# Converting a float64 weight inside an attention stage: half chunks through a spare PSUM bank, and one multiply moved from VectorE to GpSimd

## The chip, the cores and the metric

One Trainium2 chip, one of its cores. The time is device time of one launch in microseconds (us), from three runs of the kernel before: 694.91, 696.65 and 696.79, median 696.65. One more execution was profiled: it took 696.35 us, of which the profile's span covers 694.6.

## The reference, cut to what matters

The program is a chain of three blocks on a batch of 4 with 576 positions: attention with 8 heads of 64 and rotary position, then a gated feed-forward block, then a mixture of four attention experts.

```
scores = q_rot @ k_rot.T / 8                     # per batch and head, 576 x 576
attn   = exp(scores - max); attn /= sum
x      = attn @ v, heads side by side            # (4, 576, 512)
h      = gelu(x @ w_in)                          # w_in: (512, 1024), float64
u, v   = halves of h; v = layernorm(v) * g_ln
x      = x + (u * (w_sg @ v + b_sg)) @ w_out
out    = sum over the 2 experts chosen of 4 of  w_e * causal_attention_e(x)
```

The input `w_in` comes as float64. The kernel turns it into float32 itself, with integer operations on the two 32-bit words of each number, and then splits each float32 into a high and a low part, so that products on TensorE keep float32 accuracy.

## The kernel before, in words

There are three stages, one for each block. Stage 1 is the one touched. It walks through 16 *works*, one for each batch and pair of heads, and each work has nine *slots*, numbered x = 0 to 8, one for each tile of 128 query rows of the pair. A loop over k = 9n + x calls `slot(k)`, which writes the instructions of work n, slot x, and of its neighbours, in an order fixed by hand on the compute engines; on the queue of the DMA engines (SP) a scheduler may still move transfers.

In slot x TensorE makes the scores of tile x+1 (tile `ps_S`, two buffers), then turns the exponentials of tile x-1 with four transposes (`ps_t`). VectorE takes the maximum of the scores (`nmax`), ScalarE the exponential (`e`). ScalarE and VectorE share the copies of the turned tiles to SBUF (`g`). TensorE multiplies them with the values into `ps_o` in slots 1, 3, 5, 7 and 8.

576 keys are four blocks of 128 and 64 leftover keys. The leftover keys of two tiles are put side by side and turned into a bank of their own, `ps_l` (one buffer): `turn_left` in slots 4, 5 and 7, and in slots 0 and 1 of the work after. `place_left` copies the bank to SBUF (`tl`) in slot 5 and in slot 2 of the work after; the factors of the normalization pass through the same bank (`rr`). From slot 2 to slot 4 and from slot 5 to slot 7 the bank holds nothing that is still wanted.

Queries and keys of the next work are prepared beside this: rotary position on GpSimd (`rope`, tile `t`), a cast to the high part on VectorE (`hi`), the low part on GpSimd (`lo`), in slots 1 (queries) and 3 (keys), and then ten transfers that lay the parts out for TensorE (`q`, `qz`, `kh`). Scores of the next work wait for them.

In the gaps stage 1 does work for stage 2, by generators that are advanced by one step in chosen slots:

- `load_split64` (L226) converts `w_in` in eight chunks of 128 x 512 numbers. One buffer (`raw`) takes the words, one (`wt`) the result. Its steps for a chunk: an absolute value on ScalarE (L245), then on VectorE a maximum (L247), a shift left (L249), an OR with the shifted low word (L251) and an OR with the sign (L255), then the split (`wih` on ScalarE, `wil` on GpSimd) and the transfer of the next chunk. All of it lies in SBUF. The loop (L625) takes one step in slots 1, 3, 4, 6, 7 and 8 of odd works and in slot 7 of even ones.
- `attended` (L289) fetches finished attention outputs (`sa`) and their factors (`sr`), multiplies them (`norm`, L299, for batch 0 on VectorE, else on GpSimd), stores them and splits them. It takes a step in slot 8 of works 4 to 15.

Of the kernel before, what the change touches and what calls it, by code (L numbers as in the profile page):

```python
# [8 lines left out]
F32 = mybir.dt.float32  # L9
# [8 lines left out]
P = 128  # L18
# [17 lines left out]
VALUES_AT = (2, 5, 7)  # L36
FIRST_QK_AT = (0, 1, 3, 3, 4, 4)
GATES_AT = {8: 1, 9: 2, 10: 2, 11: 3}
INPUT_AT = ((0, 1, 2, 4, 6, 7), (1, 3, 5, 7), (2, 4))


@with_exitstack
def fused_kernel(ctx, tc, qk, v, w_in, w_out, w_sg, g_ln, b_sg, wqk, wvg, wo, rope, cst, out):
# [27 lines left out]
    def bank(t):  # L71
        shape = [P, 2, 512] if t.isupper() else [P, 512]
        return ps[t].tile(shape, F32, tag="b", name="ps_" + t)
# [22 lines left out]
    def split(hi, lo, src, engine=POOL):  # L96
        ACT.copy(hi, src)
        engine.tensor_tensor(lo, src, f(hi), op=ALU.subtract)
# [127 lines left out]
    def load_split64(st_pool, hi, lo, src, n0, dma, engine, bufs, scratch=None):  # L226


        def load(c):
            raw = st_pool.tile([P, 512, 2], I32, tag="raw", name="raw", bufs=bufs)  # L230
            tc.keep_in_program_order(dma(raw.rearrange("p n t -> p (n t)"), src[:, c, 2 * n0:2 * n0 + 1024]))
            return raw

        raws = ahead(load, src.shape[1]) if bufs > 1 else None
        raw = None if raws else load(0)
        for c in range(src.shape[1]):
            raw = next(raws) if raws else raw
            w0, w1 = raw[:, :, 0], raw[:, :, 1]
            def tile():
                return st_pool.tile([P, S], F32, tag="wt", name="wt", bufs=bufs)[:, 0:512]  # L240

            a = t = scratch() if scratch else tile()
            ai = a.bitcast(I32)
            yield
            ACT.activation(a, w1.bitcast(F32), AF.Abs, scale=65536.0)  # L245
            yield
            DVE.tensor_scalar(a, a, 65536.0 * TINY, None, op0=ALU.max)  # L247
            yield
            DVE.tensor_scalar(ai, ai, 3, None, op0=ALU.logical_shift_left)  # L249
            yield  # L250
            DVE.scalar_tensor_tensor(ai, w0, 29, ai, op0=ALU.logical_shift_right, op1=ALU.bitwise_or)  # L251
            yield
            if scratch:
                t = tile()
            DVE.scalar_tensor_tensor(t.bitcast(I32), w1, -2 ** 31, ai, op0=ALU.bitwise_and, op1=ALU.bitwise_or)  # L255
            yield
            split(hi[:, c, n0:n0 + 512], lo[:, c, n0:n0 + 512], t, engine)
            if not raws and c + 1 < src.shape[1]:
                raw = load(c + 1)
            yield  # L260
# [28 lines left out]
    def attended(pool, b):  # L289


        ts = {}

        def load(c):
            ts[c] = a, r = [pool.tile([P, S], F32, tag="s" + x, name="s" + x, bufs=k) for x, k in (("a", 3), ("r", 2))]
            nc.sync.dma_start(a, xraw[b][c])
            factor_in(r, rd[b][c])

        def norm(c):  # L299
            a, r = ts[c]  # L300
            (POOL if b else DVE).tensor_tensor(a, a, r, op=ALU.mult)
            nc.sync.dma_start(xd[b][c], a)

        def part(c):
            if c == 0 and b == 1:
                t = wc.tile([P, 2, 4, S], F32R, tag="w", name="x")
                xs[b] = [t[:, 0], t[:, 1]]
            elif c == 0:
                xs[b] = [pool.tile([P, 4, S], F32R, tag="x" + x, name="x" + x) for x in "hl"]
            split(*[x[:, c] for x in xs[b]], ts[c][0])  # L310

        order = (((load, 0), (norm, 0), (load, 1), (norm, 1), (load, 2), (norm, 2), (part, 0), (part, 1),
                  (part, 2), (load, 3), (norm, 3), (part, 3)) if b != 1 else
                 ((load, 0), (norm, 0), (load, 1), (norm, 1), (part, 0), (load, 2), (norm, 2), (part, 1),
                  (load, 3), (norm, 3), (part, 2), (part, 3)))
        for do, c in order:
            do(c)
            yield
# [26 lines left out]
    with ExitStack() as st:  # L345
# [180 lines left out]
        def slot(k):  # L526
# [50 lines left out]
            if nx:  # L577
# [12 lines left out]
                if x == 4 and n + 2 < B * NP:  # L590
                    works[n + 2].load_values()

        works = {0: Work(), 1: Work()}

        warm, warm2 = bank("l"), bank("o")
# [21 lines left out]
        works[0].start()  # L617
        works[0].scores(0)
        works[0].maxima(0)
        wload = itertools.chain(*[load_split64(wst, *wi, w_in, n, nc.sync.dma_start, POOL, 1) for n in (DM, 0)])  # L620
        steps = iter(())
        for k in range(9 * B * NP + 7):
            n, x = divmod(k, 9)
            slot(k)
            if x in ((1, 3, 4, 6, 7, 8) if n % 2 else (7,)):  # L625
                next(wload, None)
            if k == 9 * 4:
                steps = attended(bx, 0)
            if k == 9 * 14:
                lsteps = leftover(bx, 0)  # L630
            if n >= 4 and x == 8:
                next(steps, None)
            if n >= 14 and x == 3:
                next(lsteps, None)
            if k == 9 * 15 + 1:
                nsteps = attended(bx, 1)
            if k > 9 * 15 and x in (1, 5):
                next(nsteps, None)
# [828 lines left out]
```

## Time and profile before

| what | value |
|---|---|
| time, median of 3 runs | 696.65 us |
| the profiled execution's own time | 696.35 us |
| its span | 694.6 us |
| stage 1 | some 14 us to 284 us of the span |
| granted TensorE clock over the span | 0.994 |
| TensorE busy, by its pipelined matmuls | 97% |
| VectorE, ScalarE, GpSimd busy | 66%, 62%, 50% |

In rows of time, the first number is the start in us from the span's beginning, the second how long the row lasted; `x2` says that two like instructions were merged. In brackets stands how long the engine had sat idle before, and what ended that. PE is TensorE, DVE VectorE, ACT ScalarE, POOL GpSimd, SPq the queue of SyncE. [...]

### The profile page before, as it was taken

To read this page: it belongs to the slowest core of one execution; us is meant where nothing else is said; L and a number is where in the kernel's file an instruction comes from. 1 tells how busy PE (TensorE), PEld (TensorE's weight loads), DVE (VectorE), ACT (ScalarE), POOL (GpSimd) and SP (SyncE) were. 2 spreads that over 40 slices of the span, in tenths; PEclk is the share of its full clock that TensorE was granted. 3 is DMA by queue.
4 is the path that set the end of the run, shared out by engine and by line. 5 is a ranking of instruction groups with operands and counts; after the bars stand their busy time and mean duration, and the time that the engine had idled before them with its cause. 6 is when DMAs were issued, how large, how long until landed. Compare 5 with 4: busy or idle time off the path is not lost.

```text
span 694.6 us, 13664 instructions
## 1 busy us (share of the span) xinstructions
PE 673.4 (97%) x4781; PEld 587.9 (85%) x4781; DVE 460.3 (66%) x1015; ACT 432.2 (62%) x1046; POOL 344.7 (50%) x321
## 2 busy tenths in 40 slices
PE   7899999999999999999999999999999999999996
PEld 6777777767776777798999899899999989999875
DVE  5786868686867686478874664664247666656674
ACT  6677777767676777565571472472156686766673
POOL 1896767786878880470635317306223444242320
PEclk9899999999999999999999999999999999999999
DMA  8677878778887864461457234045455364442521
GB/s 303 176 222 204 264 237 242 216 212 243 247 230 223 236 163 133 135 189 63 121 166 215 86 98 134 17 136 151 124 167 140 91 169 101 127 127 55 151 75 68
DMA packets 65286, 112.10 MB, mean 161 GB/s; under 512 B 20513, under 2 KB 25474, under 8 KB 65218
## 3 DMA queue, kind: packets, MB, share of 16 engines
q1 hardware_dynamic: 62482, 105.55, 52.6%
q10 hardware_dynamic: 2736, 5.68, 2.8%
q8 instruction: 38, 0.62, 0.4%
q14 instruction: 30, 0.25, 0.1%
HBM read 57.96 MB, written 18.98 MB: 111 GB/s over the span
## 4 chain that ended last, share of the span: by engine, by line
PE 83%; DVE 9%; ACT 4%; DMA 2%; issue 2%; POOL 0%; SPq 0%; POOLq 0%; ACTq 0%; DVEq 0%
PE ps_S L57 45%; PE ps_o L57 16%; PE ps_t L57 13%; PE ps_f L57 5%; PE ps_s L57 3%; DVE wt L57 2%; DVE nmax L57 2%; PE ps_l L57 1%; ACT e L57 1%; ACT qz L57 1%; DVE ga L57 1%; DVE g L57 1%; DMA ws<-in_w_sg_dram 1%; DMA x<-yd 1%; ACT vh L57 0%
## 5 line engine op out<-in xcount | busy, mean ns | idle before, releaser
L57 DVE TENSOR_REDUCE nmax<-ps_S 128x1 f32<-128x576 f32 x144 | 108.1, 751 | 66.3 <-PE ps_S L57 65.2
L57 ACT ACTIVATE e<-ps_S,nmax 128x576 f32<-128x576 f32 x144 | 107.5, 746 | 69.8 <-DVE nmax L57 67.6
L57 PE MATMUL ps_t<-ident,e 128*128 128x128 f32 x776 | 122.2, 275 | 2.4 <-ACT e L57 1.4
L57 PEld LDWEIGHTS ps_t<-ident,e 128*128 128x128 f32 x776 | 95.7, 141 | 7.7 <-ACT e L57 2.6
L57 POOL TENSOR_TENSOR t<-t,rp 128x576 f32<-128x576 f32 x61 | 90.0, 1495 | 14.9 <-ACT rp L57 9.2
L57 PE MATMUL ps_S<-kh,q 128*128 128x288 f32 x352 | 86.9, 340 | 9.9 <-ACT e L57 8.2
L57 PEld LDWEIGHTS ps_S<-kh,q 128*128 128x128 f32 x352 | 53.7, 191 | 42.0 <-ACT e L57 20.1
L57 PE MATMUL ps_o<-g,v 128*64 128x320 f32 (+1 forms) x512 | 76.2, 418 | 0.0
L57 POOL TENSOR_TENSOR lo<-t,hi 128x576 fp32r<-128x576 f32 x30 | 42.8, 1427 | 51.3 <-DVE hi L57 51.3
L57 PE MATMUL ps_S<-lo,qz 128*128 128x288 f32 x304 | 66.0, 298 | 1.5 <-DVE lo L57 1.5
L57 PEld LDWEIGHTS ps_o<-g,v 128*64 128x64 f32 x512 | 31.3, 136 | 24.2 <-issue 11.3
L57 PE MATMUL ps_S<-yh,w 128*128 128x288 f32 x256 | 51.8, 304 | 0.0
L57 ACT ACTIVATE e<-e,nmax 128x128 f32<-128x128 f32 (+4 forms) x72 | 42.2, 586 | 14.3 <-DVE nmax L57 14.1
L57 PEld LDWEIGHTS ps_S<-lo,qz 128*128 128x128 f32 x304 | 49.3, 191 | 1.7 <-DVE lo L57 1.7
L57 POOL TENSOR_TENSOR yl<-x,yh 128x640 fp32r<-128x640 f32 x16 | 26.1, 1631 | 47.4 <-ACT yh L57 47.3
L57 ACT COPY g<-ps_t 128x512 f32<-128x512 f32 x80 | 46.6, 583 | 3.2 <-PE ps_t L57 2.5
L57 POOL TENSOR_TENSOR t<-t 128x576 f32<-128x576 f32 x29 | 43.5, 1500 | 2.3
L57 DVE COPY g<-ps_t 128x512 f32<-128x512 f32 x64 | 43.6, 680 | 0.1
L57 ACT ACTIVATE ga<-ga 128x512 f32<-128x512 f32 (+1 forms) x34 | 22.3, 656 | 26.6 <-DVE ga L57 26.6
L57 PEld LDWEIGHTS ps_S<-yh,w 128*128 128x128 f32 x256 | 38.8, 189 | 0.0
L57 PE MATMUL ps_S<-wsh,vh 128*128 128x288 f32 x160 | 34.6, 298 | 0.8 <-DVE u L57 0.5
L57 POOL TENSOR_TENSOR gxl<-u,gxh 128x576 fp32r<-128x576 f32 x16 | 22.8, 1435 | 24.2 <-ACT gxh L57 24.2
(281 smaller groups left out, 1777.7 us busy)
## 6 DMA issues: line engine op xcount, KB each, us to landing
t<-in_qk_dram SPq DMA_DIRECT2D x32, 576.0 KB
kh<-hi SPq DMA_DIRECT2D x92, 144.0 KB
q<-hi SPq DMA_DIRECT2D x38, 144.0 KB
qz<-hi SPq DMA_DIRECT2D x38, 144.0 KB
q<-lo SPq DMA_DIRECT2D x38, 144.0 KB
v<-in_v_dram SPq DMA_DIRECT2D x16, 320.0 KB
sa<-xr SPq DMA_DIRECT2D x16, 288.0 KB
xd<-sa SPq DMA_DIRECT2D x16, 288.0 KB
```

Of the source, the lines that this page charges most:

```text
L57: ins = op(*a, **k)
```

## The change

`w_in` is now converted by a generator of its own, `convert_in`. A chunk is still 128 x 512, but shift and ORs work on half a chunk (256 numbers) at a time and the intermediate words lie in the bank `ps_l`. The raw words have two buffers, and the next chunk is fetched right behind the absolute value. A table `W_AT` says in which slots a step is taken: a chunk begins in slots 0 to 3 of an odd work (absolute value, maximum, first half in slots 2 and 3) and ends in slots 2 to 4 of the even work behind it (second half in 2 and 3, split in 4); works 0, 1 and 15 have slots of their own. `norm` runs on GpSimd for every batch.

```
+W_AT = ((7,), (3, 4, 5, 6), (2, 3, 4), (0, 1, 2, 3), (0, 1, 2, 3, 5, 6, 7))
...
         def norm(c):
             a, r = ts[c]
-            (POOL if b else DVE).tensor_tensor(a, a, r, op=ALU.mult)
+            POOL.tensor_tensor(a, a, r, op=ALU.mult)
             nc.sync.dma_start(xd[b][c], a)
...
+        def convert_in():
+            def load(n0, c):
+                raw = wst.tile([P, 512, 2], I32, tag="raw", name="raw", bufs=2)
+                d = nc.sync.dma_start(raw.rearrange("p n t -> p (n t)"), w_in[:, c, 2 * n0:2 * n0 + 1024])
+                tc.keep_in_program_order(d)
+                return raw
+
+            todo = list(itertools.product((DM, 0), range(4)))
+            nxt = load(*todo[0])
+            yield
+            for i, (n0, c) in enumerate(todo):
+                raw = nxt
+                w0, w1 = raw[:, :, 0], raw[:, :, 1]
+                a = wst.tile([P, S], F32, tag="wt", name="wt")[:, 0:512]
+                ACT.activation(a, w1.bitcast(F32), AF.Abs, scale=65536.0)
+                if i < 7:
+                    nxt = load(*todo[i + 1])
+                yield
+                DVE.tensor_scalar(a, a, 65536.0 * TINY, None, op0=ALU.max)
+                yield
+                for h in (slice(0, 256), slice(256, 512)):
+                    t = bank("l")[:, h].bitcast(I32)
+                    DVE.tensor_scalar(t, a[:, h].bitcast(I32), 3, None, op0=ALU.logical_shift_left)
+                    DVE.scalar_tensor_tensor(t, w0[:, h], 29, t, op0=ALU.logical_shift_right, op1=ALU.bitwise_or)
+                    yield
+                    DVE.scalar_tensor_tensor(a[:, h].bitcast(I32), w1[:, h], -2 ** 31, t, op0=ALU.bitwise_and, op1=ALU.bitwise_or)
+                    yield
+                split(wi[0][:, c, n0:n0 + 512], wi[1][:, c, n0:n0 + 512], a)
+                yield
...
-        wload = itertools.chain(*[load_split64(wst, *wi, w_in, n, nc.sync.dma_start, POOL, 1) for n in (DM, 0)])
+        wload = convert_in()
...
-            if x in ((1, 3, 4, 6, 7, 8) if n % 2 else (7,)):
+            if x in W_AT[4 if n == NP * B - 1 else min(n, 2 + n % 2)]:
                 next(wload, None)
```

Two places of the order are needed below. The first is VectorE from slot 1 to slot 8 of work 3. `nmax` is the maximum of one tile of scores, `e` the leftover keys put side by side, `g` a copy of a turned tile, `hi` the cast of the next work's keys. Before:

```order
L57 TENSOR_SCALAR wt<-wt 128x512
L57 TENSOR_REDUCE nmax<-ps_S 128x1
L57 COPY g_194<-ps_t 128x4x128
L57 TENSOR_SCALAR wt<-wt 128x512
L57 TENSOR_REDUCE nmax<-ps_S 128x1
L57 TENSOR_REDUCE e<-e 128x64
L57 TENSOR_REDUCE nmax<-ps_S 128x1
L57 COPY g_195<-ps_t 128x4x128
L57 SCALAR_TENSOR_TENSOR wt<-raw,wt 128x512
L57 TENSOR_REDUCE nmax<-ps_S 128x1
L57 TENSOR_REDUCE e<-e 128x64
L57 SCALAR_TENSOR_TENSOR wt<-raw,wt 128x512
```

and now, from slot 1 to slot 4 of the same work:

```order
L58 TENSOR_SCALAR wt<-wt 128x512
L58 TENSOR_REDUCE nmax<-ps_S 128x1
L58 COPY g_194<-ps_t 128x4x128
L58 TENSOR_SCALAR ps_l<-wt 128x256
L58 SCALAR_TENSOR_TENSOR ps_l<-raw,ps_l 128x256
L58 TENSOR_REDUCE nmax<-ps_S 128x1
L58 TENSOR_REDUCE e<-e 128x64
L58 CAST hi_1031<-t_820 128x576
L58 SCALAR_TENSOR_TENSOR wt<-raw,ps_l 128x256
L58 TENSOR_REDUCE nmax<-ps_S 128x1
```

The two wide ORs behind slots 6 and 7 are gone, and three instructions of half width stand in slots 2 and 3, of this work and of the even one behind it.

The second place is SP in work 4, where `rd` is a factor's way out, `kh` the four transfers of the next keys, `v` a load of values. Before:

```order
L168 DMA qz_173<-hi_1190 64x576
L168 DMA q_1_172<-lo_1191 64x576 x2
L196 DMA rd_67<-rr 9x128
L152 DMA kh<-hi_1239 64x576 x4
L511 DMA xr_63<-xt 64x256
L511 DMA xr_63<-xt 64x64
L511 DMA xr_63<-xt 64x320
L398 DMA v<-in_v_dram 128x640
```

and now:

```order
L169 DMA qz_173<-hi_1194 64x576
L169 DMA q_1_172<-lo_1195 64x576 x2
L197 DMA rd_67<-rr 9x128
L399 DMA v<-in_v_dram 128x640
L153 DMA kh<-hi_1246 64x576 x4
L512 DMA xr_63<-xt 64x256
```

The load of values went ahead of the keys in this work; the order of TensorE in the works stays as it was.

## Rows read from the trace of the kernel before

**Rows 1.** The page: the chain that ended last, its share by engine.

```profile
PE 83%; DVE 9%; ACT 4%; DMA 2%; issue 2%; POOL 0%; SPq 0%; POOLq 0%; ACTq 0%; DVEq 0%
```

**Rows 2.** TensorE's rows of time: first scores of works 2, 3, 4, 5, 6, 15.

```profile
47.92 0.53 PE L57 MATMUL ps_S<-kh,q 128*128 128x288 f32 x2
...
65.24 0.53 PE L57 MATMUL ps_S<-kh,q 128*128 128x288 f32 x2
...
81.14 0.40 PE L57 MATMUL ps_S<-kh,q 128*128 128x288 f32 x1
...
98.48 0.40 PE L57 MATMUL ps_S<-kh,q 128*128 128x288 f32 x1
...
114.39 0.53 PE L57 MATMUL ps_S<-kh,q 128*128 128x288 f32 x2
...
264.30 0.53 PE L57 MATMUL ps_S<-kh,q 128*128 128x288 f32 x2
```

**Rows 3.** Windows: us, busy us of PE, PEld, DVE, ACT, POOL; clock; DMA.

```profile
98.48:114.39 15.91, 15.91 (x121) 12.33 (x119) 11.95 (x22) 11.37 (x30) 11.17 (x9) 1.00 0.73 209
```

**Rows 4.** VectorE's rows of time, end of work 5 and start of 6.

```profile
112.98 1.93 DVE L57 SCALAR_TENSOR_TENSOR wt<-raw,wt 128x512 int32<-128x512 int32 x1
114.83 0.74 DVE L57 TENSOR_REDUCE nmax<-ps_S 128x1 f32<-128x576 f32 x1
...
115.62 1.10 DVE L57 SCALAR_TENSOR_TENSOR wt<-raw,wt 128x512 int32<-128x512 int32 x1
...
117.92 0.74 DVE L57 TENSOR_TENSOR sa<-sa,sr 128x576 f32<-128x576 f32 x1
```

**Rows 5.** ScalarE and TensorE there, then GpSimd, rows of time.

```profile
115.67 0.74 ACT L57 ACTIVATE e<-ps_S,nmax 128x576 f32<-128x576 f32 x1 [1.72 <-DVE nmax L57]
...
116.55 0.53 PE L57 MATMUL ps_S<-kh,q 128*128 128x288 f32 x2 [0.50 <-ACT e L57]
...
112.95 3.22 POOL L57 TENSOR_TENSOR t<-t,rp 128x576 f32<-128x576 f32 x2
```

**Rows 6.** Groups by tile: count, then shortest, median and longest in ns.

```profile
L57 DVE SCALAR_TENSOR_TENSOR wt<-raw,wt x16: 681/1104/1949, 46.5 to 280.4; 128x512 int32<-128x512 int32 x16
...
L57 ACT CAST wih<-wt x8: 612/622/624, 50.3 to 281.1; 128x512 fp32r<-128x512 f32 x8
...
L57 DVE TENSOR_SCALAR ps_c<-ps_c x8: 673/696/700, 323.6 to 346.3; 128x512 f32<-128x512 f32 x4, 128x512 int32<-128x512 int32 x4
...
L57 DVE SCALAR_TENSOR_TENSOR wt<-raw,ps_c x4: 669/680/690, 328.4 to 350.0; 128x512 int32<-128x512 int32 x4
```

**Rows 7.** GpSimd's group of the factor multiply by tile: shortest, median, longest, ns.

```profile
L57 POOL TENSOR_TENSOR sa<-sa,sr x12: 1406/1436/1873, 267.7 to 419.1; 128x576 f32<-128x576 f32 x12
```

**Rows 8.** A VectorE group by form: count, then total us, mean ns.

```profile
L57 DVE CUSTOM_DVE_ANT_0 e<-ps_s,mask 128x256 f32<-128x256 f32 x16 | 6.6, 411 | 0.5 <-PE ps_s L57 0.4
```

**Rows 9.** Work 4, slots 2 to 4: VectorE, TensorE, ScalarE, in rows of time.

```profile
89.81 0.75 DVE L57 TENSOR_REDUCE nmax<-ps_S 128x1 f32<-128x576 f32 x1
...
90.60 0.45 DVE L57 CAST hi<-t 128x576 fp32r<-128x576 f32 x1
92.44 0.76 DVE L57 TENSOR_REDUCE nmax<-ps_S 128x1 f32<-128x576 f32 x1 [1.39 <-PE ps_S L57]
...
92.68 0.27 PE L57 MATMUL ps_l<-ident,e 128*128 128x128 f32 x1
...
93.32 0.74 ACT L57 ACTIVATE e<-ps_S,nmax 128x576 f32<-128x576 f32 x1 [1.17 <-DVE nmax L57]
```

**Rows 10.** Work 4, slots 6 and 7: VectorE, then TensorE, rows of time.

```profile
97.08 0.75 DVE L57 TENSOR_REDUCE nmax<-ps_S 128x1 f32<-128x576 f32 x1
...
97.27 0.27 PE L57 MATMUL ps_l<-ident,e 128*128 128x128 f32 x1
```

**Rows 11.** SP's rows of time: keys of works 3 and 5 sent off.

```profile
60.88 2.40 SPq L152 DMA_DIRECT2D kh<-hi  x4
...
92.15 2.40 SPq L152 DMA_DIRECT2D kh<-hi  x4
```

## The prediction

> **What bounds the kernel now.** I read the page first. Of the chain that ended last 83% is TensorE and 9% VectorE [rows 1], so time is to be won only where TensorE waits, and VectorE is the one to look at. Then TensorE's rows of time at the first scores of each work. From work 5 to work 6 it is 98.48 to 114.39, 15.91 us; from work 4 to work 5 it is 81.14 to 98.48, 17.34 [rows 2]. The works hold the same TensorE instructions, so one kind loses 1.43 us. In the window of the shorter one TensorE is busy for all 15.91 us [rows 3], so 15.91 is what a work costs when nothing holds TensorE. The reader is to see that the loss alternates with the conversion: behind each odd work that converts, the even one starts late.
>
> The place of the loss comes from VectorE's rows at the end of work 5. The two wide ORs take 1.93 and 1.10 us there, and the maximum that stands behind the first one starts only at 114.83 [rows 4]. ScalarE waits 1.72 us for that maximum and TensorE then 0.50 us for ScalarE [rows 5]; a second wait like it follows one slot later. So the chain is: wide OR, maximum, exponential, scores of the tile after next, which need the exponential's buffer.
>
> Over works 2 to 14 the sum of these losses is plain: 264.30 - 47.92 = 216.38 us for 13 works [rows 2], less 13 x 15.91 = 206.83, is **9.55 us**. That is what TensorE lost between these two points, whatever the reasons were. I take it as the most that the change can bring but for a few tenths in works 1 and 15.
>
> **What is removed.** Eight chunks lose two wide ORs each on VectorE, median 1.10 and up to 1.95 us [rows 6]. They are slow because both inputs lie in SBUF while GpSimd works there: GpSimd's two products beside the first OR took 3.22 us [rows 5], and the same kind of OR with one input in PSUM took 669 to 690 ns every time [rows 6].
>
> [...]
>
> Four multiplies of 0.74 us leave VectorE for GpSimd, one of them in front of the start of work 6 [rows 4]. On GpSimd one takes 1.44 us [rows 7]; GpSimd is busy 11.17 of 15.91 us [rows 3], and in odd works the new multiply takes the place of the split that goes to the even work. I cost it at nothing. If GpSimd had no room, the low part of the queries would be late by 1.44 us, and their transfers with it; that is in the first rival.
>
> **What is added, and what hides it.** Each work from 2 to 14 now has three instructions of half width on VectorE, two in slot 2 and one in slot 3. The trace shows none of these. Bounds: half of a wide one, 0.34, and all of it, 0.69 [rows 6]. A VectorE instruction of 256 elements that reads PSUM took 411 ns [rows 8]; I take **0.41**, so three cost 1.23 us.
>
> [...]
>
> Does it hold TensorE? I walk through slots 2 to 4 of work 4 [rows 9]. The maximum at 89.81 starts 0.82 later, at 90.63; the cast of the keys moves from 90.60 to 91.42, ends at 91.87, and the third half instruction ends at 92.28. Two things wait for it. The next maximum had to wait for scores until 92.44 anyway (VectorE sat idle for 1.39 us there). And TensorE turns the next leftover keys into the same bank at 92.68, which now has to wait until the bank has been read: 0.40 us to spare. The exponential delayed by 0.82 us is not what TensorE waits for in the next scores, since VectorE's wait ahead of 92.44 was for TensorE and not the other way. So the cost is **0**, with 0.40 us of cover; at 0.34 each there is more, at 0.69 each the third instruction ends at 93.12, 0.44 late, and 15 such works cost 6.6 us.
>
> ScalarE's split cast moves to slot 4 of the even works, into 1.17 us of idle time ahead of 93.32 [rows 9]; it takes 0.62 us [rows 6], so it costs nothing. The absolute value moves by one slot and costs as much as before.
>
> Works 1 and 15 put halves into slots 5 and 6. There the maximum at 97.08 stands directly behind a copy; the half instruction comes between, from 97.08 to 97.49, and TensorE wants the bank at 97.27 [rows 10]. That is a new wait of 0.22 us, and with the signal some 0.25; two of them cost **0.5 us**.
>
> **The transfers that are moved.** Keys leave SP as four issues of 0.60 us each [rows 11], behind the cast. The cast comes 0.82 us later, and in works 2, 4 and 12 the load of values now goes ahead of them, one more issue, so another 0.60. In work 4 the last issue ended at 94.55 and the first use is at 98.48 [rows 2, 11], 3.93 us. How long a landing takes no row shows, but work 2 bounds it: issues ended at 63.28 and TensorE used the keys at 65.24 in full stride [rows 2, 11], so 1.96 us suffice. Work 4 thus has 1.97 us in hand, and 0.55 after both delays. For work 2 the trace proves no spare time. But there the transfer of raw words goes out of the way, to the front of odd works. I cost the transfers at 0 and keep the loss as a rival.
>
> **Sum.** 9.55 - 0.5 = 9.05 us. The profiled execution took 696.35 us, span 694.6; 696.35 - 9.05 = **687.3 us**. It lies 0.3 us below the median of the runs, 696.65, which is inside their spread. After stage 1 nothing changes but that all starts sooner.
>
> **Rivals.**
> - *Keys come late.* For it: the proven spare is nil in work 2, and the cast is later in every work. Against it: 1.97 us in hand in work 4. If the three works with the load of values ahead pay both delays, 3 x 1.42 = 4.3 us are lost: 691.6. If every one of 14 works paid 0.82, it would be 11.5 us, and no gain.
> - *The bank holds TensorE in every work (ends slower).* The place is the turn at 92.68 [rows 9], which now waits for VectorE's third half instruction. If these cost what the wide ones do in SBUF, 1.10 each [rows 6], it would end at 94.35, 1.67 us late; 15 x 1.67 = 25 us, and 696.35 - 9.55 + 25 = 711.8. It decides from where the lateness times 15 exceeds 9.55, that is 0.64 us, or 2.27 us for the three instead of 1.23. Against it: the rows with one input in PSUM never exceeded 0.69, and three of those make 2.07.
> - *Half of that.* With each at the full-width price of 0.69 it is 6.6 us back: 693.9 or so.
> - *The change doesn't do what it says.* The wait of TensorE could be ScalarE's, with the maximum only seeming to end it, or GpSimd's products might now end too late. Then 9.55 shrinks to nothing: 696. Against it: VectorE's row at 114.83 begins where the wide OR ends.
>
> **Chances.** Forecast (8 to 10.5 us gained) 0.70; keys late or bank at the dear price with some gain left (2.1 to 8 us) 0.20; no effect 0.05; slower by the bank 0.05. A difference of 0.3%, 2.1 us, is about what can be told from none here. So faster 0.90, same 0.05, slower 0.05. The range: below, all 9.55 us and half a microsecond from works 1 and 15, off a run as low as the lowest of before (694.91) gives 684.9. Above, the first rival's 691.6. Some 1.5 in 10 lie outside.
>
> **What would show it.** Right: starts of works 15.9 us apart from work 2 on; VectorE's half instructions at 0.4 us without long ones among them; no idle time of TensorE with ScalarE's exponential behind it at the start of even works; idle time of 0.2 to 0.3 us before a turn into `ps_l` in works 1 and 15 alone. Wrong: idle time before that turn in every work with VectorE behind it (the bank), or before the first scores of a work with a transfer of `kh` behind it (late keys), or works that still alternate between 15.9 and 17.3.

## The result and the profile after

The changed kernel took 687.95 us (median of 4 runs, 687.48 to 688.58) against 696.44 of the kernel before on the same chip (4 runs): ratio 0.988, 95% interval 0.9854 to 0.9906. Its profiled execution took 687.48 us, where 687.3 was forecast. The granted TensorE clock is the same in both (0.994 before, 0.995 now). Faster by 1.2%, and the forecast was right in sign, in size and in the waits that went; the price of the multiply's move and two smaller terms were not, and one reason it gave for the gain turned out to be only half of it.

The page's chain of waits, as in [rows 1], now reads so (lines of the changed kernel are one higher, L58 for L57):

```profile
PE 87%; DVE 5%; ACT 3%; DMA 1%; issue 1%; POOL 1%; SPq 0%; ACTq 0%; DVEq 0%; POOLq 0%
```

VectorE's share fell from 9% to 5%, TensorE's rose from 83% to 87%. The starts of works 2, 3, 4, 5, 6 and 15 from TensorE's rows of time, against [rows 2]:

```profile
47.71 0.53 PE L58 MATMUL ps_S<-kh,q 128*128 128x288 f32 x2
...
63.61 0.40 PE L58 MATMUL ps_S<-kh,q 128*128 128x288 f32 x1
...
79.51 0.40 PE L58 MATMUL ps_S<-kh,q 128*128 128x288 f32 x1
...
95.41 0.40 PE L58 MATMUL ps_S<-kh,q 128*128 128x288 f32 x1
...
111.31 0.40 PE L58 MATMUL ps_S<-kh,q 128*128 128x288 f32 x1
...
255.06 0.53 PE L58 MATMUL ps_S<-kh,q 128*128 128x288 f32 x2
```

The alternation between 15.9 and 17.3 us is gone: each of these works takes 15.90. From work 2 to work 15 it is 207.35 us where it was 216.38, so 9.03 of the 9.55 us named as the loss came back. The window of work 5 (columns as in [rows 3]) shows where the multiply and the split went: GpSimd is now busy 12.52 us of 15.90 instead of 11.17, and TensorE still all the time.

```profile
95.41:111.31 15.90, 15.90 (x120) 12.32 (x118) 12.02 (x25) 11.56 (x31) 12.52 (x10) 1.00 0.75 216
```

The groups by tile that answer to [rows 6] (count, then shortest, median and longest in ns):

```profile
L58 DVE TENSOR_SCALAR ps_l<-wt x16: 408/416/427, 43.8 to 267.4; 128x256 int32<-128x256 int32 x16
L58 DVE SCALAR_TENSOR_TENSOR ps_l<-raw,ps_l x16: 428/432/450, 44.3 to 267.9; 128x256 int32<-128x256 int32 x16
L58 DVE SCALAR_TENSOR_TENSOR wt<-raw,ps_l x16: 408/412/416, 45.9 to 269.6; 128x256 int32<-128x256 int32 x16
```

All 48 half instructions lie between 408 and 450 ns; the wide ORs of before reached 1949. Slots 2 to 4 of work 4, against [rows 9], in rows of time of VectorE and then of TensorE:

```profile
86.74 0.42 DVE L58 TENSOR_SCALAR ps_l<-wt 128x256 int32<-128x256 int32 x1
87.19 0.44 DVE L58 SCALAR_TENSOR_TENSOR ps_l<-raw,ps_l 128x256 int32<-128x256 int32 x1
87.53 0.75 DVE L58 TENSOR_REDUCE nmax<-ps_S 128x1 f32<-128x576 f32 x1
88.20 0.21 DVE L58 TENSOR_REDUCE e<-e 128x64 f32<-128x64 f32 x1
88.32 0.45 DVE L58 CAST hi<-t 128x576 fp32r<-128x576 f32 x1
88.69 0.41 DVE L58 SCALAR_TENSOR_TENSOR wt<-raw,ps_l 128x256 int32<-128x256 int32 x1
89.37 0.76 DVE L58 TENSOR_REDUCE nmax<-ps_S 128x1 f32<-128x576 f32 x1 [0.27 <-PE ps_S L58]
...
89.61 0.27 PE L58 MATMUL ps_l<-ident,e 128*128 128x128 f32 x1
```

VectorE's rows overlap a little: the second half instruction's runs to 87.63, and the maximum behind it starts at 87.53. The third half instruction ends at 89.10, the next maximum still waits for scores (0.27 us), and the turn into the bank at 89.61 has no idle time before it: 0.51 us of cover where 0.40 was worked out. In works 1 and 15, where halves stand in slots 5 and 6, the turn does wait, as answer to [rows 10]:

```profile
46.47 0.30 PE L58 MATMUL ps_l<-ident,e 128*128 128x128 f32 x1 [0.20 <-DVE wt L58]
...
270.11 0.30 PE L58 MATMUL ps_l<-ident,e 128*128 128x128 f32 x1 [0.20 <-DVE wt L58]
```

The 0.52 us by which 207.35 exceeds 13 x 15.91 were not in the forecast. Works 11 and 13 took 16.16 and 16.17, and work 9 took 16.04 (15.90 in a second execution of the same kernel). In work 11 it begins with the cast of the queries, VectorE's row and GpSimd's beside it:

```profile
195.83 1.43 DVE L58 CAST hi<-t 128x576 fp32r<-128x576 f32 x1
...
195.53 1.41 POOL L58 TENSOR_TENSOR xl<-sa,xh 128x576 fp32r<-128x576 f32 x1
```

The median cast takes 0.45 us. Here it lasted 1.43 beside a product of GpSimd, the split of an attended output. That product starts 4.60 us into the work now and 2.58 before, since the split of the weights moved to the even works and goes ahead of it. Everything behind the cast on VectorE is late, and the period is 0.26 us longer. Five more casts took 0.70 to 1.42 us, all beside a product of GpSimd; of these only the one in work 13 made its work longer.

### The profile page after: what moved, and what is told of

It reads as the page before. It is cut to its first block, busy times and chain, and to the rows that moved or that the text cites. A ratio compares the mean times of both kernels' runs of the same rounds, so it can differ in the third digit from the quotient of the medians.

```text
span 685.3 us, 13688 instructions
## 1 busy us (share of the span) xinstructions
PE 670.0 (98%) x4781; PEld 588.3 (86%) x4781; DVE 455.1 (66%) x1035; ACT 428.2 (62%) x1046; POOL 342.6 (50%) x325
## 4 chain that ended last, share of the span: by engine, by line
PE 87%; DVE 5%; ACT 3%; DMA 1%; issue 1%; POOL 1%; SPq 0%; ACTq 0%; DVEq 0%; POOLq 0%
PE ps_S L58 47%; PE ps_o L58 17%; PE ps_t L58 14%; PE ps_f L58 5%; PE ps_s L58 3%; PE ps_l L58 2%; ACT qz L58 1%; DVE nmax L58 1%; ACT e L58 1%; DMA x<-yd 1%; DMA sa<-xr 0%; POOL sa L58 0%; POOL x L58 0%; DVE ga L58 0%; POOL wsl L58 0%
## 5 line engine op out<-in xcount | busy, mean ns | idle before, releaser
L58 ACT ACTIVATE e<-ps_S,nmax 128x576 f32<-128x576 f32 x144 | 107.9, 749 | 70.2 <-DVE nmax L58 69.7
L58 DVE TENSOR_REDUCE nmax<-ps_S 128x1 f32<-128x576 f32 x144 | 108.6, 754 | 57.5 <-PE ps_S L58 55.2
L58 PE MATMUL ps_t<-ident,e 128*128 128x128 f32 x776 | 121.8, 275 | 2.4 <-ACT e L58 1.4
L58 PEld LDWEIGHTS ps_t<-ident,e 128*128 128x128 f32 x776 | 95.4, 141 | 7.6 <-ACT e L58 2.4
L58 POOL TENSOR_TENSOR t<-t,rp 128x576 f32<-128x576 f32 x61 | 85.4, 1420 | 14.2 <-ACT rp L58 9.2
L58 PE MATMUL ps_S<-kh,q 128*128 128x288 f32 x352 | 87.7, 342 | 3.7 <-ACT kh L58 2.1
L58 PEld LDWEIGHTS ps_S<-kh,q 128*128 128x128 f32 x352 | 54.4, 192 | 32.3 <-ACT g L58 10.3
L58 PE MATMUL ps_o<-g,v 128*64 128x320 f32 (+1 forms) x512 | 76.2, 418 | 0.0
L58 PE MATMUL ps_S<-lo,qz 128*128 128x288 f32 x304 | 66.3, 300 | 1.5 <-DVE lo L58 1.5
L58 POOL TENSOR_TENSOR lo<-t,hi 128x576 fp32r<-128x576 f32 x30 | 43.2, 1441 | 48.8 <-DVE hi L58 48.8
L58 PEld LDWEIGHTS ps_o<-g,v 128*64 128x64 f32 x512 | 31.3, 136 | 24.2 <-issue 9.5
L58 PE MATMUL ps_S<-yh,w 128*128 128x288 f32 x256 | 51.9, 305 | 0.0
L58 PEld LDWEIGHTS ps_S<-lo,qz 128*128 128x128 f32 x304 | 49.7, 192 | 1.7 <-DVE lo L58 1.7
L58 ACT ACTIVATE e<-e,nmax 128x128 f32<-128x128 f32 (+4 forms) x72 | 42.2, 586 | 14.2 <-DVE nmax L58 13.9
L58 POOL TENSOR_TENSOR yl<-x,yh 128x640 fp32r<-128x640 f32 x16 | 26.1, 1631 | 47.7 <-ACT yh L58 47.6
L58 ACT COPY g<-ps_t 128x512 f32<-128x512 f32 x80 | 46.7, 584 | 2.4 <-PE ps_t L58 1.7
L58 DVE COPY g<-ps_t 128x512 f32<-128x512 f32 x64 | 43.5, 680 | 1.4 <-PE ps_t L58 1.3
L58 POOL TENSOR_TENSOR t<-t 128x576 f32<-128x576 f32 x29 | 41.3, 1426 | 2.3
L58 PEld LDWEIGHTS ps_S<-yh,w 128*128 128x128 f32 x256 | 38.8, 189 | 0.0
L58 ACT ACTIVATE ga<-ga 128x512 f32<-128x512 f32 (+1 forms) x34 | 22.3, 657 | 25.7 <-DVE ga L58 25.7
L58 PE MATMUL ps_S<-wsh,vh 128*128 128x288 f32 x160 | 34.7, 298 | 0.8 <-DVE u L58 0.5
L58 POOL TENSOR_TENSOR gxl<-u,gxh 128x576 fp32r<-128x576 f32 x16 | 22.7, 1429 | 25.3 <-ACT gxh L58 25.3
```

The source lines that it names most:

```text
L58: ins = op(*a, **k)
```

## The experiments

Two theories stood against each other. **A**: the ORs are fast because one input lies in PSUM, which keeps them clear of GpSimd. **B**: they are fast because of the place; in slots 2 and 3 GpSimd is idle, and PSUM does nothing. GpSimd's row of the changed kernel in work 4 shows the idle time, 3.17 us before 88.91, in which the first two half instructions lie:

```profile
88.91 1.42 POOL L58 TENSOR_TENSOR lo<-t,hi 128x576 fp32r<-128x576 f32 x1 [3.17 <-DVE hi L58]
```

A third question was how thin the cover of the bank is, and a fourth what the multiply contributes.

"2 to 15" below is the time from the first scores of work 2 to those of work 15, read from TensorE's rows of each trace. Ratios are against the kernel before on the same chip.

| kernel | median us | ratio, 95% interval | 2 to 15, us |
|---|---|---|---|
| before | 696.44 | | 216.38 |
| changed | 687.95 | 0.9880 (0.9854 to 0.9906) | 207.35 |
| e1 halves in SBUF | 687.69 | 0.9895 (0.9855 to 0.9936) | 207.11 |
| e2 wide in SBUF | 688.69 | 0.9909 (0.9874 to 0.9943) | 207.59 |
| e3 wide in PSUM | 691.59 | 0.9956 (0.9939 to 0.9973) | 209.60 |
| e4 two more shifts | 710.47 | 1.0213 (1.0163 to 1.0262) | 222.78 |
| e5 slots 5 and 6, PSUM | 692.63 | 0.9989 (0.9978 to 1.0000) | 211.86 |
| e6 slots 5 and 6, SBUF | 695.27 | 1.0032 (1.0020 to 1.0044) | 214.77 |
| e7 attempt at better | 687.75 | 0.9923 (0.9909 to 0.9936) | 207.16 |
| e8 changed again | 688.43 | 0.9928 (0.9914 to 0.9941) | 207.27 |
| e9 multiply alone | 696.62 | 1.0006 (0.9987 to 1.0024) | 217.07 |
| e10 conversion alone | 692.09 | 0.9937 (0.9922 to 0.9952) | 211.40 |
| e11 no bank, one raw buffer | 690.69 | 0.9923 (0.9904 to 0.9943) | 211.12 |

The medians of the kernel before lie between 693.0 and 696.4 us on the chips used (e1 to e4 ran on one, e5 to e8 on a second, e9 and e10 on a third), so kernels of different chips are compared by their traces. The two traces of the changed kernel, the second one being e8, differ by 0.08 us from 2 to 15.

**e1: the halves in SBUF.**

```diff
-                    t = bank("l")[:, h].bitcast(I32)
+                    t = wst.tile([P, 256], I32, tag="wh", name="wh")
```

> The changed kernel with one edit: the intermediate words of a half lie in SBUF instead of the bank of the leftover keys. Place, order and widths stay. Theory A (PSUM matters: a VectorE instruction with two SBUF inputs is held up by GpSimd, one with an input in PSUM is not): the two ORs of a half, 0.41 to 0.45 us each now, show long cases of 0.7 to 1.0 beside GpSimd's low part of the keys, which begins in slot 3 beside the third half instruction; the maximum behind it has 0.27 us to spare, so up to 0.3 us in some 14 works is lost and the time is 689 to 692. Theory B (only the place matters: in slots 2 and 3 GpSimd is idle and VectorE has time): the ORs stay at 0.41 to 0.45, the period stays 15.90, and the two waits of 0.20 us for the bank in works 1 and 15 go: 687.0 to 687.7 against 687.5 of the changed kernel's profiled execution.

Measured: 687.69 us, the same as the changed kernel; the period is 15.90 in works 3 to 10. In slots 2 and 3 the two ORs took 0.42 us each, here in work 4:

```profile
87.26 0.28 DVE L58 TENSOR_SCALAR wh<-wt 128x256 int32<-128x256 int32 x1
87.57 0.42 DVE L58 SCALAR_TENSOR_TENSOR wh<-raw,wh 128x256 int32<-128x256 int32 x1
...
89.08 0.42 DVE L58 SCALAR_TENSOR_TENSOR wt<-raw,wh 128x256 int32<-128x256 int32 x1
```

So theory A, as a reason for the gain at this place, falls. Only work 1, whose first half stands in slots 5 and 6, shows the other side. VectorE and then GpSimd in e1:

```profile
44.08 0.71 DVE L58 TENSOR_SCALAR wh<-wt 128x256 int32<-128x256 int32 x1
44.82 1.59 DVE L58 SCALAR_TENSOR_TENSOR wh<-raw,wh 128x256 int32<-128x256 int32 x1
...
44.71 1.42 POOL L58 TENSOR_TENSOR t<-t 128x576 f32<-128x576 f32 x1
```

The OR starts 0.11 us behind GpSimd's product and ends 0.28 behind that product's end at 46.13; it lasted 1.59 us, where the same OR takes 0.42 in work 4. The same two instructions of the changed kernel, with the intermediate in the bank, beside the same product (44.46 to 45.88 there):

```profile
43.82 0.41 DVE L58 TENSOR_SCALAR ps_l<-wt 128x256 int32<-128x256 int32 x1
44.27 0.43 DVE L58 SCALAR_TENSOR_TENSOR ps_l<-raw,ps_l 128x256 int32<-128x256 int32 x1
```

Work 1 comes out alike in both (16.33 and 16.29 us): what the bank's wait costs there, the hold-up costs in SBUF. But VectorE is still late at the start of work 2, which takes 16.12 us in e1 and 15.90 in the changed kernel, so the hold-up costs more than the wait.

**e2: full width in SBUF, at the new place.**

```diff
-W_AT = ((7,), (3, 4, 5, 6), (2, 3, 4), (0, 1, 2, 3), (0, 1, 2, 3, 5, 6, 7))
+W_AT = ((7,), (3, 4, 5, 6), (4,), (0, 1, 2, 3), (0, 1, 2, 3, 5))
-                for h in (slice(0, 256), slice(256, 512)):
-                    t = bank("l")[:, h].bitcast(I32)
+                for h in (slice(0, 512),):
+                    t = a[:, h].bitcast(I32)
```

> The changed kernel with shift and ORs at full width, all in SBUF as before the change, but at the changed kernel's place: slots 2 and 3 of odd works, nothing of it but the split in the even ones. Raw words in two buffers and the multiply on GpSimd stay. It is the change of place by itself. Theory A (two SBUF inputs are slow because of GpSimd wherever they stand): wide ORs with a median near 1.10 and up to 1.95 us as before; the three then take up to 3.5 us in slots 2 and 3 where 1.9 us are free on VectorE, and 0.5 to 1.5 us is lost in each of 7 odd works: 691 to 697. Theory B (place): the wide ORs take 0.68 to 0.75, the loss per odd work is 0 to 0.4 us: 687 to 690.

Measured: 688.69 us. The group of the wide ORs:

```profile
L58 DVE SCALAR_TENSOR_TENSOR wt<-raw,wt x16: 676/688/1803, 45.6 to 265.7; 128x512 int32<-128x512 int32 x16
```

The median fell from 1104 ns [rows 6] to 688 by the place alone. The longest, 1803, is again the one in slot 5 of work 1. Odd works from 3 on lose 0.06 to 0.09 us; works 1 and 2, behind the slow OR, take 16.69 and 16.39. Theory B holds: neither the halving nor the bank is needed for most of the gain.

**e3: full width through the bank.**

```diff
-W_AT = ((7,), (3, 4, 5, 6), (2, 3, 4), (0, 1, 2, 3), (0, 1, 2, 3, 5, 6, 7))
+W_AT = ((7,), (3, 4, 5, 6), (4,), (0, 1, 2, 3), (0, 1, 2, 3, 5))
-                for h in (slice(0, 256), slice(256, 512)):
+                for h in (slice(0, 512),):
```

> The changed kernel with shift and ORs at full width through the bank, in slots 2 and 3 of odd works alone, the split in slot 4 of the even ones. It tests the cover that the prediction put at 0.40 us. Three instructions of 0.69 us instead of 0.41 to 0.45 make the third end 0.8 us later, near 89.9 in the time of work 4 where TensorE turns the next leftover keys into the bank at 89.61. Theory A with the cover as predicted: TensorE waits 0.3 to 0.5 us for VectorE before that turn in each of 7 odd works, none in even ones: 2 to 3.5 us lost, 689.5 to 691. Theory C (the bank's lateness is taken up by other idle time of TensorE's, or the cover is larger): no period above 15.95, 687 to 688.

Measured: 691.59 us, a little over the expected upper end. The third instruction and the turn in work 3, VectorE and TensorE:

```profile
74.14 0.68 DVE L58 SCALAR_TENSOR_TENSOR wt<-raw,ps_l 128x512 int32<-128x512 int32 x1
...
74.88 0.33 PE L58 MATMUL ps_l<-ident,e 128*128 128x128 f32 x1 [0.20 <-DVE wt L58]
```

Each odd work from 3 to 13 is 0.41 to 0.45 us longer than 15.90, or more: 16.72 in work 9, where the next first scores wait besides. The prediction had said 0.44 late for instructions of 0.69 us. The idle time in the row is only 0.20 of it. A matmul's end is modelled: in both kernels the row of the transposes ahead of the turn lasts 0.60 us, yet in work 3 of the changed kernel the turn starts 0.43 behind their start, and in e3 0.80. What a wait costs is therefore read from starts, here and in the works. In work 1, in slots 5 and 6, it is 1.16 us.

**e4: two more shifts in each half.**

```diff
-                    DVE.tensor_scalar(t, a[:, h].bitcast(I32), 3, None, op0=ALU.logical_shift_left)
+                    for _ in range(3):
+                        DVE.tensor_scalar(t, a[:, h].bitcast(I32), 3, None, op0=ALU.logical_shift_left)
```

> The changed kernel with each half's shift done three times (the same result): 0.90 us more on VectorE ahead of the third half instruction, in every work from 2 to 14. It prices the rival that the bank holds TensorE in every work. With a cover of 0.4 to 0.5 us the turn into the bank is 0.4 to 0.5 us late in each of 13 to 15 works: 5 to 7.5 us lost, 692.5 to 695, and an idle time of TensorE of that size with VectorE behind it before the turn in slot 4. If the cover is larger than the half instructions let one see (other waits shrink), less than 2 us is lost; if lateness adds up through VectorE (maximum, exponential, scores), more than 9, and the gain is gone.

Measured: 710.47 us, slower than the kernel before, far outside the 692.5 to 695 expected. The price of the bank was as expected: the slot with the turn is 0.55 us longer in every work from 2 to 14 (1.45 in work 11), some 8 us in all. What was not expected is another 8 us at the last slot of the works, 1.46 us in work 4, 2.05 in work 6, 1.00 in work 12 and so on. It is the first scores of the next work that wait there. TensorE at the start of work 7, and SP's issue of its keys:

```profile
135.41 0.50 PE L58 MATMUL ps_S<-kh,q 128*128 128x288 f32 x2 [1.98 <-DMA xr<-xt]
...
128.47 2.89 SPq L153 DMA_DIRECT2D kh<-hi  x4
```

The last of the four issues ended at 131.36 and the scores began 4.05 us later, released by a transfer. The bracket names an output transfer that was issued right behind the keys; the signals of the first two key transfers are among those that these scores wait for, and in the trace they come last at 134.83 and 135.16, just ahead of 135.41. In the changed kernel 2.45 us of issues for work 3 from 58.06 led to scores at 63.61 without idle time. So the prediction's first rival, late keys, is real: it begins somewhere within 0.9 us of the cast's place in the changed kernel, and then costs as much as the bank.

**e5 and e6: slots 5 and 6 in every work, in PSUM and in SBUF.** The table for e5, and for e6 the edit of e1 besides:

```diff
-W_AT = ((7,), (3, 4, 5, 6), (2, 3, 4), (0, 1, 2, 3), (0, 1, 2, 3, 5, 6, 7))
+W_AT = ((7,), (3, 4, 5, 6), (5, 6, 7), (3, 4, 5, 6), (0, 1, 2, 3, 5, 6, 7))
```

> The changed kernel with its half instructions in slots 5 and 6 of every work instead of 2 and 3 (the chunk begins in slots 3 and 4 of odd works, the split is in slot 7 of even ones): the bank is free there too, but GpSimd's rotary products run beside them. In the first run of this study a half OR with SBUF inputs took 1.59 us there, in work 1. Theory A (an instruction with one input in PSUM is not held up by GpSimd): all 48 half instructions stay at 0.41 to 0.45 us; what is lost is the wait for the bank before the turn in slot 7, 0.20 us as in works 1 and 15, in each of 13 works, so 2 to 4 us more than the changed kernel: 689.5 to 692. Rival (GpSimd's products hold them up in PSUM as well): half instructions of 0.7 to 1.6 us, TensorE idle for 0.5 to 1.5 us before the turn: 695 to 705.

> The same place as the run beside it, slots 5 and 6 of every work, but the intermediate words in SBUF. Theory A: beside GpSimd's products a half shift takes up to 0.7 and a half OR with two SBUF inputs up to 1.6 us; VectorE is 0.5 to 1.4 us late in slots 5 to 7 of each of 13 works, and half of that or more reaches TensorE, as in the kernel before, where wide ORs of 1.1 and 1.9 us cost 1.43 us per pair of works: 693 to 705. Theory B in its strong form (the place decides by VectorE's free time alone, not by GpSimd): the two take 0.28 and 0.42 us, there is no wait for a bank, and the time is 687 to 689.

Here GpSimd's rotary products run beside the halves. The groups of e5, then of e6:

```profile
L58 DVE TENSOR_SCALAR ps_l<-wt x16: 410/422/428, 43.9 to 271.9; 128x256 int32<-128x256 int32 x16
L58 DVE SCALAR_TENSOR_TENSOR ps_l<-raw,ps_l x16: 428/430/434, 44.3 to 272.4; 128x256 int32<-128x256 int32 x16
L58 DVE SCALAR_TENSOR_TENSOR wt<-raw,ps_l x16: 410/410/411, 45.9 to 274.1; 128x256 int32<-128x256 int32 x16
```

```profile
L58 DVE TENSOR_SCALAR wh<-wt x16: 282/712/1035, 44.1 to 274.7; 128x256 int32<-128x256 int32 x16
L58 DVE SCALAR_TENSOR_TENSOR wh<-raw,wh x16: 424/1593/1604, 44.9 to 275.1; 128x256 int32<-128x256 int32 x16
L58 DVE SCALAR_TENSOR_TENSOR wt<-raw,wh x16: 408/409/867, 47.6 to 277.3; 128x256 int32<-128x256 int32 x16
```

This bears out the hold-up of theory A: with the intermediate in PSUM no instruction was held up here, 48 of 48 within 410 to 434 ns, 42 of them beside a product of GpSimd; with all of it in SBUF the shift goes from 0.28 to 0.71 and the OR from 0.42 to 1.59 us. In this place the bank is worth 2.9 us (211.86 against 214.77; 2.6 by the medians, on the same chip), although each work pays 0.39 us for its wait (period 16.30). The expectation had 0.20, the idle time in the row, and so e5, at 692.63 us, ended a little above its 689.5 to 692; e6, at 695.27, lies in its 693 to 705. Both are much slower than the same instructions in slots 2 and 3.

Not only instructions with two SBUF inputs were long beside GpSimd: the shift, with one, took 282 ns at the shortest and 712 in the median in e6 (1.03 us at 93.17, beside products that ran from 91.25 to 94.05), and the cast of work 11 in the changed kernel 1.43 us where the median is 0.45.

**e9 and e10: the multiply alone, and the conversion alone.**

```diff
 # e9, in the kernel before
-            (POOL if b else DVE).tensor_tensor(a, a, r, op=ALU.mult)
+            POOL.tensor_tensor(a, a, r, op=ALU.mult)
 # e10, in the changed kernel
-            POOL.tensor_tensor(a, a, r, op=ALU.mult)
+            (POOL if b else DVE).tensor_tensor(a, a, r, op=ALU.mult)
```

> The kernel before with the second part of the change alone: the factor multiply of batch 0 on GpSimd instead of VectorE (it stands ahead of the starts of works 6, 8, 10 and of slot 0 of work 15). The prediction put no gain of its own to it, since it took the loss of 9.55 us as a whole. The trace of before shows works 5, 7 and 9 losing 0.18 us more around it than the others. If that is this multiply's share: 0.4 to 0.8 us gained, which only the trace can tell from nothing, and the alternation between 15.9 and 17.3 us stays. Rival (the multiply carries much of the loss, since it stands behind the slow ORs): 2 us or more gained. Other rival (GpSimd has no room in those works): its products end 1.4 us later, the ORs beside them are slow for longer, and the time rises by 1 to 3 us.

> The changed kernel with the factor multiply of batch 0 back on VectorE, 0.74 us each, four of them. Where the conversion no longer fills VectorE there, the multiply finds idle time: 0 to 0.7 us lost, all of it around the starts of works 6, 8, 10 and 15. If the move to GpSimd was what made room: 2 us or more lost. It also tells whether the 0.25 us in works 11 and 13 hang on GpSimd's load: if they go, GpSimd had too much to do there.

Alone, the multiply's move brings nothing that the time shows (ratio 1.0006); the conversion alone brings only 0.6%, and both together 1.2%. In e10 works 6, 8 and 10 take 17.24, 17.28 and 17.28 us. VectorE's group and one of its rows in work 6, with GpSimd and TensorE there:

```profile
L58 DVE TENSOR_TENSOR sa<-sa,sr x4: 750/1934/1953, 114.1 to 261.9; 128x576 f32<-128x576 f32 x4
```

```profile
114.10 1.91 DVE L58 TENSOR_TENSOR sa<-sa,sr 128x576 f32<-128x576 f32 x1
115.94 0.74 DVE L58 TENSOR_REDUCE nmax<-ps_S 128x1 f32<-128x576 f32 x1
...
113.98 1.42 POOL L58 TENSOR_TENSOR t<-t 128x576 f32<-128x576 f32 x1
...
116.86 0.33 PE L58 MATMUL ps_l<-ident,e 128*128 128x128 f32 x1 [1.12 <-DVE e L58]
```

In the kernel before this multiply came at 117.92 and took 0.74 [rows 4]. With the conversion out of its way it comes earlier, falls beside a rotary product and takes 1.91: two SBUF inputs, the same hold-up as the ORs had, and TensorE stands still behind it. Its move to GpSimd is worth 4.05 us of the 9.03 (211.40 to 207.35). The expectation had 0 to 0.7, and its second case, 2 us or more, came out. Its question on works 11 and 13 is answered too: they still take 16.23 and 16.19 us with the multiply back on VectorE, and the cast of work 11 takes 1.52. So those losses don't hang on the multiply.

In e9 works 6, 8 and 10 gain the 0.18 us each, 0.5 in all, but work 14 takes 17.32 instead of 16.07 us. The wide OR at the end of work 13 and GpSimd's product, before and then in e9:

```profile
246.82 0.68 DVE L57 SCALAR_TENSOR_TENSOR wt<-raw,wt 128x512 int32<-128x512 int32 x1
...
246.81 3.80 POOL L57 TENSOR_TENSOR t<-t,rp 128x576 f32<-128x576 f32 x2
```

```profile
246.34 1.94 DVE L57 SCALAR_TENSOR_TENSOR wt<-raw,wt 128x512 int32<-128x512 int32 x1
...
246.33 3.22 POOL L57 TENSOR_TENSOR t<-t,rp 128x576 f32<-128x576 f32 x2
```

In both traces GpSimd's row starts 0.01 us ahead of VectorE's, and yet in one GpSimd's pair is the longer (3.80, with the OR at 0.68), in the other the OR (1.94, with the pair at 3.22). Within the trace of before, too, an OR at 79.73 with the same 0.01 between the two took 1.95. What decided isn't shown; it moved this work by 1.25 us, and the gain of 0.5 in e9 is hidden behind it.

**e11: without the two new resources.** Halves in SBUF as in e1, one buffer for the raw words, filled in a step of its own behind the split.

```diff
-W_AT = ((7,), (3, 4, 5, 6), (2, 3, 4), (0, 1, 2, 3), (0, 1, 2, 3, 5, 6, 7))
+W_AT = ((7,), (3, 4, 5, 6), (2, 3, 4, 5), (0, 1, 2, 3), (0, 1, 2, 3, 5, 6, 7))
-                raw = wst.tile([P, 512, 2], I32, tag="raw", name="raw", bufs=2)
+                raw = wst.tile([P, 512, 2], I32, tag="raw", name="raw")
...
                 ACT.activation(a, w1.bitcast(F32), AF.Abs, scale=65536.0)
-                if i < 7:
-                    nxt = load(*todo[i + 1])
...
                 split(wi[0][:, c, n0:n0 + 512], wi[1][:, c, n0:n0 + 512], a)
                 yield
+                if i < 7:
+                    nxt = load(*todo[i + 1])
+                yield
```

> The changed kernel without its two new resources: the intermediate halves lie in SBUF, and the raw words have one buffer again, filled behind the split in slot 5 of even works. What is left of the change is the place of the steps and the multiply on GpSimd. If these two carry the gain, as the factorial pair of runs with the multiply alone (no gain) and the place alone (some 4 us) says, the period stays at 15.90 us but for works 1, 11 and 13, and the time is 687 to 689. If the second buffer matters (the absolute value in slot 0 waits for raw words fetched only three slots ahead, or the transfer collides with the keys), ScalarE waits for them in odd works and 0.3 us or more is lost in each: over 690.

Measured: 690.69 us, and 211.12 from 2 to 15, 4.0 more than e1. ScalarE's absolute value and SP's issue of the raw words for work 5:

```profile
101.78 0.66 ACT L58 ACTIVATE wt<-raw 128x512 f32<-128x512 f32 x1 [1.52 <-DMA raw<-in_w_in_dram]
...
97.86 0.38 SPq L599 DMA_DIRECT2D raw<-in_w_in_dram  x1
```

The issue left SP only behind the keys and three output transfers, and the words were there 3.9 us later; ScalarE waited 1.52 us with the next exponential queued behind it. Five odd works lose 0.5 to 1.4 us each. With two buffers the words are fetched a chunk ahead, and ScalarE shows no such wait. So with the transfer at this place the second buffer is needed. Whether one buffer would do with an earlier place on SP was not tried.

**e7 and e8: an attempt at a better version, and the changed kernel beside it.** e7 gives works 1 and 15 the regular slots and moves three splits of attended outputs away from the converted weights' product:

```diff
-W_AT = ((7,), (3, 4, 5, 6), (2, 3, 4), (0, 1, 2, 3), (0, 1, 2, 3, 5, 6, 7))
+W_AT = ((3,), (0, 1, 2, 3), (2, 3, 4), (0, 1, 2, 3), (0, 1, 2, 3))
+        if b == 0:
+            order = ((load, 0), (norm, 0), (load, 1), (norm, 1), (load, 2), (norm, 2), (part, 0), (load, 3),
+                     (norm, 3), (part, 1), (part, 2), (part, 3))
-            if n >= 4 and x == 8:
+            if n >= 4 and x == 8 and n != 10 or k == 9 * 14 + 3:
```

> An attempt at a better version: the changed kernel with the regular slots in works 1 and 15 as well (no half instruction in slots 5 and 6 any more, the last chunk ends behind work 15), and the attended outputs of batch 0 split at other times (in works 11, 14, 14 and 15 instead of 10, 11, 12 and 15), so that GpSimd's product of that split no longer stands beside the product of the converted weights in even works. By the trace of the changed kernel 0.39 us were lost in work 1, 0.25 in each of works 11 and 13 and 0.25 around work 15: 0.8 to 1.2 us less than the changed kernel in the same call, starts of works 15.90 us apart from work 1 on but for work 9. If the idle times there have another cause, nothing is gained; if the weights that come later delay the second stage, it is slower by up to 2 us.

> The changed kernel itself once more, unedited, on the same chip as the run before it and for comparison with it: 687 to 688.5, a period of 15.90 us in works 2 to 8, and 0.25 us lost in each of works 11 and 13.

Measured: 687.75 (686.96 to 689.11) and 688.43 us (687.38 to 688.87); 0.8 to 1.2 us less were expected, and the two cannot be told apart by time. By the traces, from the start of work 1 to that of work 15, it is 223.08 against 223.57 us, and work 15 takes 15.90 against 16.29 (to the next transposes), 0.88 in all. Works 1, 11 and 13 take 15.93, 15.90 and 15.90 in e7, so those three losses had the causes named; the cast of work 11 is back at its price:

```profile
195.88 0.46 DVE L58 CAST hi<-t 128x576 fp32r<-128x576 f32 x1
```

But work 2 takes 16.39. SP's issue of the keys of work 3, and TensorE's first scores there:

```profile
59.71 2.39 SPq L153 DMA_DIRECT2D kh<-hi  x4
...
63.79 0.50 PE L58 MATMUL ps_S<-kh,q 128*128 128x288 f32 x2 [0.42 <-ACT e L58]
```

The keys leave 12.31 us behind the start of work 2, where the changed kernel has 10.35. The bracket names an exponential that the same scores did not wait for in the changed kernel; the signal of the second key transfer comes last at 63.55. About a third of what was won (0.48 of some 1.35 us) is lost at the thinnest place of the keys.

## Why the prediction came out, step by step

- **The loss of 9.55 us between works 2 and 15** was the right ceiling and the right reading of the rows: 9.03 came back. But to take the ORs away would not have brought it back alone. By e10 the new conversion alone gives 4.98 us (216.38 to 211.40), and the multiply's move the other 4.05, since on VectorE the multiply is held up in its turn. Alone the move gives 0.18 us in each of three works, so the two parts have no separate prices.
- **What is removed: two inputs in SBUF beside GpSimd.** That this holds ORs up is shown by e5 and e6, which differ only in where the intermediate lies: the first OR of a half took 0.43 us with it in PSUM and 1.59 with it in SBUF (medians). As the reason for this gain it was only half: in slots 2 and 3 GpSimd is idle, and the ORs are just as fast there in SBUF (0.42 us in e1; 688 ns at full width in e2).
- **The multiply on GpSimd at nothing.** This term was mis-sized: with the conversion gone from its old place the move is worth 4.05 us (e10), since on VectorE the multiply would have gone from 0.74 to 1.91 us. The sum came out only because both parts were made together. Missed besides was that the weights' split, moved to the even works, pushes another split beside a cast (1.43 us in place of 0.45, 0.5 us in works 11 and 13 together; e10 shows that this isn't the multiply's doing, and e7 takes it away). The prediction looked at the ORs alone; what GpSimd would do to the casts and to a multiply left on VectorE was not looked at.
- **Half instructions at 0.41 us**: 0.41 to 0.43, right.
- **The cover of 0.40 us** before the turn: 0.51, and e3 and e4 confirm that being late has a price, 0.43 us in an odd work where 0.44 was worked out. That these two agree is partly luck: the cover was 0.11 larger, and some 0.1 from the last half instruction's end to TensorE's going on was not counted.
- **Works 1 and 15, 0.25 us each**: the waits are there, but each work lost 0.39 (16.29 us, against 15.90 before in work 1 and in e7 in work 15). The term was undersized, since the idle time in a row (0.20 us) is less than what the work loses. The 0.03 us in it for the signal were the author's estimate, which no row gave; in work 1 the turn at 46.47 starts 0.15 us behind the end of the half instruction (45.91 and 0.41).
- **Transfers at 0**: right, but nearer to the edge than the 0.55 us in hand suggested. e4 and e7 each met late keys.
- **The rival that ends slower** was real as a mechanism and only far off in place: e4 needs 0.9 us more per half to end slower. Its point of decision, 0.64 us of lateness per work (over 15 works; the changed order has 13 such), was too high. At 0.55 the bank's loss of 8 us is doubled by keys that come late with it.
- **The sum**, 687.3 against 687.48 of the profiled execution, is better than its parts, and that is luck: 0.52 us of new losses in works 9, 11 and 13 were not in it, nor were the dearer works 1 and 15, and the start of work 1, 0.60 us earlier in this execution than in the one before (31.42 against 32.02; 32.06 in e8), made up for most of them. Up to the end of work 15 it is 9.03 - 0.39 - 0.22 + 0.60 = 9.02 us (work 15 took 16.07 before and 16.29 now); the two executions differ by 8.87.

## What to carry to other kernels

When VectorE's instructions have several lengths, look at what GpSimd runs beside the long ones before changing how they compute: moving them to a place where GpSimd is idle gave the same here with and without the intermediate in PSUM (207.35 and 207.11 us), and more than PSUM gave beside GpSimd (211.86), where there is a bank to wait for. Then walk the other instructions that touch SBUF alone on both engines through the new order, since whatever takes the old place can be held up in its turn; here a multiply nobody had called slow was worth 4 of 9 us. And a step that is free where it stands has a margin to two or three waits at once: test it by doubling it.

## What the runs showed of the hardware

- A VectorE instruction with two SBUF inputs that started just behind a GpSimd product ended 0.3 to 0.6 us after that product (46.41 against 46.13 in e1, 116.01 against 115.40 in e10): 0.42 became 1.59 us at half width (e1, e6), 0.68 became 1.94 (e9), 0.74 became 1.91 (e10). A shift with one SBUF input went from 0.28 to 0.71 and up to 1.04 us (e6), a cast from 0.45 to 1.43 (work 11 of the changed kernel).
- With the intermediate in PSUM the same instructions showed no such case: in e5 42 of 48 ran beside a GpSimd product, in the changed kernel 18 of 48, and all took 408 to 450 ns. The shift alone is slower there when nothing disturbs it: 0.42 us (changed kernel) against 0.28 (e1).
- Which of the two engines takes longer can't be read from starts 0.01 us apart: with the same order of starts the OR took 0.68 us in one place (before, 246.82) and 1.94 or 1.95 in two others (e9 at 246.34, before at 79.73), and it moved a work by 1.25 us.
